# Retention of the last two batches in 64-token chunks, short units in one stretch, instruction pages in the planner, and more of v's scaling on ScalarE

## The chip, the cores and the metric

The kernel runs on one core of one Trainium2 chip. The metric is the device time of an execution in microseconds (us). The kernel before takes 283.19 us, the median of three runs (283.08 to 283.52).

The core's engines each have a queue of their own and run it in order: TensorE (PE, whose weight loads are listed apart as PEld), VectorE (DVE), ScalarE (ACT), GpSimd (POOL) and SyncE (SP). DMAs are issued from POOL, SP and ACT and are carried out by 16 DMA engines. Products of PE land in PSUM, which has eight banks; everything else is held in SBUF.

## The reference

```python
batch, n_heads, seq, head_dim = (8, 8, 576, 64)
n_tokens, d_model, d_ff = (4608, 512, 2048)

scores = scale * np.matmul(q, k.transpose(0, 1, 3, 2))      # scale = 1/sqrt(64)
gamma = 1.0 - 2.0 ** (-5.0 - np.arange(H, dtype=np.float32))
Dmat = np.where(rel >= 0, gamma[:, None, None] ** rel[None, :, :], 0.0)   # rel = pos_i - pos_j
ret = scores * Dmat[None, :, :, :]
x = np.matmul(ret, v)             # then (batch, seq, heads*head_dim) as 4608 rows of 512
h = x @ w_in
g = 0.5 * h * (1.0 + erf(h * inv_sqrt2))
out = g @ w_out
```

So there are two stages: retention (attention with a decay in place of a softmax, causal), and an MLP of two layers with an exact gelu. All inputs and the output are float32; the kernel multiplies in bfloat16 and sums in float32.

## The kernel before, in words

**Units and blocks.** The 576 tokens of a batch are four chunks of 128 and a tail of 64. A unit is one chunk of one batch; two batches make a pair (`bp`, 0 to 3), and the two units of a pair at the same chunk `ci` form a group. The tails of the two batches of a pair share one short unit. There are 36 units; four of them make a block of 512 tokens, and the MLP runs over nine blocks.

**Retention of a unit.** Because the decay is a power of the distance, a chunk needs only its own scores and a state `u` (64x64 for each head) of what came before. The steps on PE are: the transposes of q and k (the first units; later ones come by a transposing DMA from SP), `scores` (L583), `inner` (L644: masked scores times v), `state` (L673: adds k times v, scaled, to the state in PSUM), and `cross` (L690: state times q). On the other engines are `masked` (L612: scores times a mask on DVE), `scaled_v` (L630: v times a decay for each head, on DVE in one instruction or on ACT in eight), `u_copy` (L685: the state from PSUM to SBUF) and `evacuate` (L701: the result times a decay into `xT`, the MLP's input). Units with `ci` 0 (`raw`) use a full decay mask and the unscaled v, and need no cross product. With 128-token chunks the scores are a 128x128 square for each head, of which the mask removes what lies above the diagonal. With 64 rows and 64 columns to a product, PE can hold four of them in its four quarters at a time.

**The MLP.** The first layer of a block is done in four parts `kp`; three of these are "units" of seven half-size products each (a Strassen-like scheme, `unit` L957, order `PRODUCTS`) and one is plain (`mlp1` L914). `LAYOUTS` says which, and how they interleave. The second layer uses the same scheme (`fast` L972, order `SECOND`), but for block 0, which is plain. In the last block each row group `r` has its own chain of additions and its own stores (L1182): one store of half width when product 3 is in, and one of full width when products 5 and 4 are in. A store of the row group that holds the short unit goes out as two DMAs of 64 rows, since its rows belong to two batches.

**What sets the order.** The program is written straight out by a planner that runs when the kernel is built (`Plan`, L30). Each operation has a cost, a due time, dependencies, and the rings and PSUM banks that it needs; the planner keeps a clock for each engine and takes the operation that can start first. PE's work comes in three classes: single retention steps at the start, "macros" (`macro_of`, L1230: the inner, state and cross steps of a group and the scores of the next, one after the other in a stretch), and MLP pieces in between (`pe_candidates`, L1333). Groups in `APART` have their scores in a macro of their own. Up to 16 us of its own clock the planner fills gaps of PE with dummy products (`warm`, L1307). The loads are issued by POOL in the order of `ORDER`, with at most eight on their way.

**The numbers that the change touches** are the lists at L172 to L193: `VH_ACT` (units whose v is scaled on ACT; 36 and 37 name no unit), `LAYOUTS`, `ORDER`, `PRODUCTS`, `SECOND`, and the due times.

Of the kernel before, what the change touches and what calls it, by code (L numbers as in the profile page):

```python
# [9 lines left out]
FP32 = mybir.dt.float32  # L10
# [97 lines left out]
def kernel(  # L108
# [41 lines left out]
    raw = [i for i in range(N_U) if units[i][1] == 0]  # L150
    old = [0, 1, 2, 3]
    tails = list(tail_of.values())
# [6 lines left out]
    def slot_of(i):  # L159
# [12 lines left out]
    VH_ACT = [15, 18, 23, 24, 25, 34, 36, 37]  # L172
# [5 lines left out]
    VH_DUE = 14.0  # L178
    FAST = 1
    APART = [6, 7]  # L180
    BEFORE = 5.5
    UNIT_FROM = 2
    LOOK = 6
    HOLD = 5.5
    LAYOUTS = {2: ['0', '12', 'p3'], 3: ['23', '0', 'p1'], 4: ['0', '12', 'p3'], 5: ['2', '30', 'p1'], 6: ['2', '30', 'p1'], 7: ['2', '30', 'p1'], 8: ['0', '12', 'p3']}
    LEAD = 9.2
    SPREAD = 5.7
    EASE = 9
    ORDER = ("k3 v1 q3 k1 q1 wi0 v3 k2 q2 wi5 wi4 pos wi1 wi6 wi2 k5 v2 wi3 wo0 k4 q5 wi7 q4 v4 v5 wo4 v6 wo1 wo5 "
             "wo2 wo6 k6 k10 wo7 v7 k7 q8 q6 wo3 q9 q7 k9 v8 v10 k8 v9 q10").split()  # L190
    K_ORDER = [0, 1, 8, 9, 2, 3, 10, 11, 4, 5, 12, 13, 6, 7, 14, 15]
    PRODUCTS = "3251476"
    SECOND = "1267543"  # L193
# [21 lines left out]
    DRAIN = 0.21  # L215

# [106 lines left out]
    step = const.tile([128, HP, 1], FP32, name="step")  # L323
    val = const.tile([128, 1, 128], FP32, name="val")
# [50 lines left out]
    add("step", "act", 0.2, ["lg", "near7"], lambda: nc.scalar.activation(step, lgT, AF.Exp, scale=float(C)), 5.0)  # L375
    add("args", "dve", 0.45, ["pos", "lg"], make_args, 8.0)
# [6 lines left out]
    add("warm_act", "act", 1.45, ["dv", "step", *(f"dq1.{hp}" for hp in range(HP))],  # L383
        lambda: nc.scalar.activation(warm_act, ln_scale, AF.Gelu), 13.7)
    DQ = {1: [f"dq1.{hp}" for hp in range(HP)], 2: ["dq2"], 3: ["dq3"], 4: ["dq4"]}
# [114 lines left out]
    def make_dq(i):  # L500
        n = min(C, S - i * C)
        nc.vector.tensor_tensor(dqT[:, :, i * C:i * C + n], dqT[:, :, (i - 1) * C:(i - 1) * C + n],
                                step.to_broadcast([128, HP, n]), op=ALU.mult)
# [18 lines left out]
    for i in (2, 3, 4):  # L522
        add(f"dq{i}", "dve", 0.6, DQ[i - 1] + ["step"], lambda i=i: make_dq(i), (0, 0, 24.0, 34.0, 40.0)[i])

# [35 lines left out]
    def turn(i, jj):  # L560
        b, t = st[i]["tr", jj] = bank([128, HP, 128], BF16, "qk_ps")
        for hp in range(HP):
            nc.tensor.transpose(t[:, hp, :], part_of(i, jj)[0][:, 2 * hp:2 * hp + 2, :], ident1)  # L563
        read(i, f"turn{jj}")
# [17 lines left out]

    def scores(i):  # L583
        if i in old:
            qkT = qkT_of(i)
            got = [bank([128, HP, 128], FP32, f"sc{e}") for e in range(2)]
            for hp in range(HP):
                for e in range(2):
                    sl = slice(64 * e, 64 * e + 64)
                    nc.tensor.matmul(got[e][1][:, hp, :], lhsT=qkT[sl, 1, hp, :], rhs=qkT[sl, 0, hp, :],  # L590
                                     start=True, stop=True)
        elif i in tails:
            qkT = qkT_of(i)
            got = [bank([128, H, TAIL], FP32, f"sc{e}") for e in range(2)]
            for h in range(H):
                for e in range(2):
                    sl = slice(64 * e, 64 * e + 64)
                    nc.tensor.matmul(got[e][1][sl, h, :], lhsT=qkT[sl, 1, h, :], rhs=qkT[sl, 0, h, :], start=True, stop=True)  # L598
        else:
            qkT, n = qkT_of(i), i - slot_of(i)  # L600
            got = [bank([128, HP, 128], FP32, f"sc{e}") for e in range(2)]
            for hh in range(HP):
                h = 4 * n + hh
                for half in range(2):
                    out_ = slice(64 * half, 64 * half + 64)
                    for e in range(2):
                        sl = slice(64 * e, 64 * e + 64)
                        nc.tensor.matmul(got[e][1][out_, hh, :], lhsT=qkT[sl, 1, h, out_], rhs=qkT[sl, 0, h, :],  # L608
# [3 lines left out]
    def masked(i, e):  # L612
# [4 lines left out]
        rows = slice(64 * e, 64 * e + 64) if i in tails else slice(0, 128)  # L617
        shape = [128, H, TAIL] if i in tails else [128, HP, 128]
        r = st[i]["ret", e] = ret_pool.tile(shape, BF16, tag=f"ret{e}", name=f"ret{e}")
# [827 lines left out]
```

## Time and profile before

| | |
|---|---|
| median of three runs | 283.19 us |
| profiled execution | 282.95 us |
| its span, from the first to the last instruction | 281.0 us |
| PE busy | 274.9 us (98%), 3531 products |
| DVE busy | 239.2 us (85%) |
| ACT busy | 154.0 us (55%) |
| POOL busy | 110.4 us (39%) |
| granted clock of PE, mean | 0.998 |
| retention on PE: scores L608, inner L661, state L679, cross L698 | 9.0, 7.6+2.9, 6.8, 6.3 us busy |

A row of the timeline gives the start in us from the span's start, the length of the merged piece, engine, line, operation, tiles, shapes and the count of instructions; in square brackets stands how long the engine was idle before and what released it. The digits of the page are shares of busy time in 40 equal slices of 7.0 us, in tenths. Products of PE are pipelined and their ends are modelled, so lengths of neighbouring rows overlap: the time that a row takes is read from its start to the next one's start. The rows of the waits are: who waited, for whom, us in total, how many times, the longest.

### The profile page before, as it was taken

How to read it: one execution, taken by the hardware profiler on the slowest of the kernel's cores; microseconds unless marked ns; L12 is line 12 of the kernel's file. 1: busy time of each engine (PE TensorE's matmuls, PEld its weight loads, DVE VectorE, ACT ScalarE, POOL GpSimd, SP SyncE). 2: the span in 40 equal slices, each digit the busy share in tenths (PEclk: the TensorE clock that was granted, in tenths of full speed). 3: DMA queues.
4: the chain of work that ended last, by engine and by line, in shares of the span. 5: the costliest groups of instructions: out<-in, count | busy, mean ns of one | idle time of the engine just before them, and what ended most of it. 6: DMA issues, size and time to landing. Idle time of an engine off the chain costs nothing.

```text
span 281.0 us, 8429 instructions
## 1 busy us (share of the span) xinstructions
PE 274.9 (98%) x3531; PEld 220.5 (78%) x3531; DVE 239.2 (85%) x457; ACT 154.0 (55%) x339; POOL 110.4 (39%) x139
## 2 busy tenths in 40 slices
PE   7999999999999999999999999999999999999994
PEld 2589848678888688868886888688868886888783
DVE  3780693799999999999999989999999999959932
ACT  7578505455318942893188467732683458227740
POOL 8967769807946096601454713425000000000000
PEclk9999999999999999999999999999999999999999
DMA  9999999999999999999999999999900040012013
GB/s 147 161 193 180 184 179 162 190 127 200 128 150 171 196 124 123 133 220 135 165 199 89 154 146 205 48 125 147 212 1 3 2 152 2 0 51 101 2 37 112
DMA packets 152068, 35.53 MB, mean 126 GB/s; under 512 B 141024, under 2 KB 147680, under 8 KB 152032
## 3 DMA queue, kind: packets, MB, share of 16 engines
q0 software_dynamic: 115792, 17.97, 96.2%
q1 hardware_dynamic: 35200, 16.78, 32.8%
q8 instruction: 27, 0.44, 0.7%
q10 hardware_dynamic: 1040, 0.26, 0.4%
q14 instruction: 9, 0.07, 0.1%
HBM read 36.70 MB, written 9.44 MB: 164 GB/s over the span
## 4 chain that ended last, share of the span: by engine, by line
PE 92%; DVE 3%; DMA 2%; issue 0%; ACT 0%; POOL 0%; POOLq 0%
PE oT L980 33%; PE hT L920 18%; PE zT L962 10%; PE yT L962 7%; PE oT L937 5%; PE o_ps L661 3%; PE sc L608 3%; DMA qk_ld<-in_k_dram 2%; PE qk_ps L563 2%; PE u_ps L679 1%; PE warm L1312 1%; PE o_ps L698 1%; DVE s L827 1%; PE sc L590 1%; PE sc L598 0%; DVE ret L627 0%
## 5 line engine op out<-in xcount | busy, mean ns | idle before, releaser
L920 PE MATMUL hT<-xT,w_in 128*128 128x128 bf16 (+2 forms) x496 | 57.8, 269 | 0.0
L980 PEld LDWEIGHTS <-g 128*128 128x128 bf16 x512 | 49.5, 98 | 7.2
L927 ACT ACTIVATE g<-hT 128x512 bf16<-128x512 f32 (+1 forms) x76 | 38.1, 513 | 22.2 <-PE hT L920 20.6
L920 PEld LDWEIGHTS <-w_in 128*128 128x128 bf16 x496 | 37.5, 98 | 12.4
L962 PEld LDWEIGHTS <-wi_sum 128*128 128x128 bf16 x420 | 41.1, 98 | 6.4
L488 POOL DMA_DIRECT2D qk_ld<-in_q_dram x31 | 27.9, 901 | 44.1 <-DMA qkT<-qk_ld 25.0
L980 PEld LDWEIGHTS <-s 128*128 128x128 bf16 x384 | 37.1, 98 | 5.0 <-issue 0.3
L627 DVE TENSOR_TENSOR ret<-sc,msk 128x512 bf16<-128x512 f32 (+1 forms) x56 | 36.2, 680 | 1.8 <-PE sc L608 1.3
L488 POOL DMA_DIRECT2D v_ld<-in_v_dram x31 | 28.2, 911 | 10.9 <-ACT vh L640 7.2
L980 PE MATMUL oT<-w_sum,s 128*128 128x256 bf16 x256 | 31.1, 273 | 0.2 <-ACT o_sb L1068 0.2
L1068 ACT COPY o_sb<-oT 128x512 f32<-128x512 f32 (+1 forms) x27 | 14.4, 539 | 29.7 <-PE oT L980 16.2
L980 PE MATMUL oT<-w_sum,g 128*128 128x256 bf16 x256 | 30.6, 273 | 0.0
L488 POOL DMA_DIRECT2D qk_ld<-in_k_dram x31 | 28.3, 912 | 4.4 <-DMA v_ld<-in_v_dram 2.3
L980 PE MATMUL oT<-w_out,g 128*128 128x256 bf16 x256 | 29.8, 273 | 0.0
L1037 ACT ACTIVATE g<-zT 128x512 bf16<-128x512 f32 x42 | 24.3, 610 | 2.2 <-DVE zT L1046 1.5
L1072 DVE TENSOR_TENSOR o_sb<-o_sb,oT 128x512 f32<-128x512 f32 (+1 forms) x27 | 16.7, 623 | 9.5 <-ACT o_sb L1068 5.4
L538 DVE COPY qkT<-qk_ps 128x512 bf16<-128x512 bf16 x17 | 6.8, 419 | 17.3 <-PE qk_ps L563 17.2
L637 DVE TENSOR_TENSOR vh<-v_ld,dv 128x512 bf16<-128x512 bf16 x30 | 20.2, 681 | 1.5 <-DMA v_ld<-in_v_dram 1.5
L962 PEld LDWEIGHTS <-w_in 128*128 128x128 bf16 x168 | 16.4, 98 | 2.1
L540 ACT COPY q<-yT 128x512 f32<-128x512 f32 x13 | 7.5, 593 | 17.3 <-PE yT L962 17.3
L716 DVE TENSOR_TENSOR xT<-o_ps,dqT 128x512 bf16<-128x512 f32 x24 | 15.3, 679 | 0.5 <-PE o_ps L698 0.5
L937 PE MATMUL oT<-w_out,g 128*128 128x512 bf16 x64 | 15.5, 380 | 0.0
(175 smaller groups left out, 472.4 us busy)
## 6 DMA issues: line engine op xcount, KB each, us to landing
out_dram<-o_sb SPq DMA_DIRECT2D x30, 256.0 KB, 3.2
qk_ld<-in_k_dram POOLq DMA_DIRECT2D x31, 128.0 KB, 6.8
v_ld<-in_v_dram POOLq DMA_DIRECT2D x31, 128.0 KB, 7.8
qk_ld<-in_q_dram POOLq DMA_DIRECT2D x31, 128.0 KB, 6.8
w_in<-in_moe_w_in_dram POOLq DMA_DIRECT2D x8, 256.0 KB, 8.5
w_out<-in_moe_w_out_dram POOLq DMA_DIRECT2D x8, 256.0 KB, 8.2
out_dram<-o_sb SPq DMA_DIRECT2D x12, 128.0 KB, 2.8
qk_ld<-in_k_dram POOLq DMA_DIRECT2D x8, 64.0 KB, 6.5
```

The source lines that it names most:

```text
L488: nc.gpsimd.dma_start(dst, src[2 * bp + j, :, ci * C:ci * C + C, :].rearrange("h s d -> s h d"))
L627: nc.vector.tensor_tensor(r[rows], t[rows], by, op=ALU.mult)
L637: nc.vector.tensor_tensor(vh, loaded[i][1], dv[:, :, ci:ci + 1].to_broadcast([128, H, D]), op=ALU.mult)
L716: nc.vector.tensor_tensor(dst, o, dqT[:, :, ci * C:ci * C + C], op=ALU.mult)
L920: nc.tensor.matmul(hT[:, m, :], lhsT=w[:, cc, o:o + 128], rhs=x_of(t)[:, cc, lo:hi], start=(cc == 0), stop=(cc == N_DM - 1))
L927: nc.scalar.activation(g_of(t, m0)[:, m0 % 2:m0 % 2 + n, m0 // 8, lo:hi], hT, AF.Gelu)
L937: nc.tensor.matmul(oT, lhsT=g_of(t, m)[:, m % 2, m // 8, ts * 128:ts * 128 + 128], rhs=w_out_sb[m // 2][:, m % 2, :], start=(n == 0), stop ...
L962: nc.tensor.matmul(c[:, m, :], lhsT=unit_left(kp, p, m)[:, cc, :], rhs=unit_right(t, p)[:, cc, :], start=(p in "321" and m + cc == 0), sto ...
L980: nc.tensor.matmul(c[:, at, :], lhsT=left(t, p, kp)[:, kk, r * 128:r * 128 + 128], rhs=right(p, kp)[:, kk, :], start=(p in OPENS and at + ...
L1037: nc.scalar.activation(target(key, what), chain[key][n][1], AF.Gelu)
L1068: nc.scalar.copy(target(key, what), chain[key][n][1])
L1072: nc.vector.tensor_tensor(to, to, chain[key][n][1], op=ALU.add)
```

## The change

1. *Fine units.* The units of the last batch pair (`FINE = 3`) are worked in two halves of 64 tokens. Scores, inner, cross and state products are all 64x64 with 64 columns; the half above the diagonal is left out. The state is copied twice a chunk: after the first half (`u..,0`) and after the second (`u..,1`). Each chunk is two macros: (a) the inner products between the two halves, the first half of the state update and half of the next group's scores, (b) the inner products within each half, all cross products, the second half of the state update and the other half of the next group's scores. `weave` writes the products of two lists, one for the upper and one for the lower 64 rows of the array, in turn. Between macros the planner keeps `GAP_A` or `GAP_B` of 1.6 us. A chunk needs two masks in place of four. Chunk 0 of this pair is no longer `raw`: its v is the scaled one, it is evacuated by DVE with a decay table `dq0`, which one more instruction on each of ACT and DVE makes.
2. *Short units* have one bank for their scores and one mask; inner and cross are one woven stretch (`in_t`).
3. *Pages.* The planner counts products; every 127.8 of them it holds PE's clock until 3.5 us (6.2 while the planner has a DMA moving) after the last page began.
4. *ScalarE scales v* of 20 units in place of 6, each in four parts of two heads in place of two parts of four.
5. The lists are others: `ORDER` (the position table of POOL third, unit 1's k and v behind the first weights), `LAYOUTS` (three parts by the seven-product scheme and one plain in every block, as before), `PRODUCTS` and `SECOND` with the last two exchanged, and due times.

```diff
+    FINE = 3
+    fine = [i for i in range(N_U) if units[i][0] >= FINE and units[i][2] is not None]
+    raw = [i for i in range(N_U) if units[i][1] == 0 and i not in fine]
...
-    VH_ACT = [15, 18, 23, 24, 25, 34, 36, 37]
+    VH_ACT = [5, 6, 7, 8, 9, 10, 16, 17, 19, 20, 23, 25, 27, 29, 30, 31, 32, 33, 34, 35, 36, 37]
...
+    PARTS = 4
     FAST = 1
+    FETCH = 3.5
+    BUSY_FETCH = 6.2
+    GAP_A = 1.6
+    GAP_B = 1.6
     APART = [6, 7]
-    BEFORE = 5.5
+    BEFORE = 3.7
     UNIT_FROM = 2
     LOOK = 6
-    HOLD = 5.5
-    LAYOUTS = {2: ['0', '12', 'p3'], 3: ['23', '0', 'p1'], 4: ['0', '12', 'p3'], 5: ['2', '30', 'p1'], 6: ['2', '30', 'p1'], 7: ['2', '30', 'p1'], 8: ['0', '12', 'p3']}
-    LEAD = 9.2
-    SPREAD = 5.7
+    HOLD = 5.0
+    LAYOUTS = {2: ['0', '12', 'p3'], 3: ['0', '12', 'p3'], 4: ['01', '2', 'p3'], 5: ['01', '2', 'p3'], 6: ['23', '0', 'p1'], 7: ['0', '12', 'p3'], 8: ['0', '12', 'p3']}
+    LEAD = 8
+    SPREAD = 6.7
     EASE = 9
-    ORDER = ("k3 v1 q3 k1 q1 wi0 v3 k2 q2 wi5 wi4 pos wi1 wi6 wi2 k5 v2 wi3 wo0 k4 q5 wi7 q4 v4 v5 wo4 v6 wo1 wo5 "
-             "wo2 wo6 k6 k10 wo7 v7 k7 q8 q6 wo3 q9 q7 k9 v8 v10 k8 v9 q10").split()
+    ORDER = ("q1 q2 pos k2 q3 k3 v3 wi0 k1 wi4 v2 v1 wi5 wi1 wi2 wi3 wi6 v4 k5 wi7 q5 q4 wo0 k4 v5 wo4 wo1 wo5 wo2 "
+             "q9 wo6 q6 wo7 v10 v7 q8 k7 v6 wo3 k6 v9 q7 k10 k9 v8 k8 q10").split()
...
-    PRODUCTS = "3251476"
-    SECOND = "1267543"
+    PRODUCTS = "3251467"
+    SECOND = "1267534"
...
+    PAGE, PAGE_AT = 127.8, 92
+    page = [0, 0.0]
+
+    def paged():
+
+        while made[0] > PAGE_AT + page[0] * PAGE:
+            T["pe"] = max(T["pe"], page[1] + (BUSY_FETCH if any(m.start <= T["pe"] < m.end - 1.0 for q_ in moving.values() for m in q_) else FETCH))
+            page[:] = page[0] + 1, T["pe"]
...
+    def scores_atoms(n, b):
+        qkT, sc, rows = qkT_of(n), st[n]["sc", b][1], half(b)
+        if n in tails:
+            return [(N64, [(sc[rows, h, :], qkT[rows, 1, h, :], qkT[rows, 0, h, :], True, True)]) for h in range(H)]
+        return [(N64, [(sc[half(t), h, :], qkT[rows, 1, h, half(t)], qkT[rows, 0, h, half(t)], True, True) for t in range(2)])
+                for h in range(H)]
...
+    def weave(names):
...
+        order, took = [], 0.0
+        for r, atoms in enumerate(lists_of(names)):
+            at = 0.0
+            for lasts, products in atoms:
+                order.append((at, r, products))
+                at += lasts
+            took = max(took, at)
+        waits_for = {fences[nm] for nm in names if nm in fences}
+        for n, (_, _, products) in enumerate(sorted(order, key=lambda o: o[:2])):
+            for out_, w, x, begin, ends in products:
+                last_on_pe[0] = product(out_, lhsT=w, rhs=x, start=begin, stop=ends, skip_group_check=True)
+                for one in waits_for:
+                    tc.add_manual_dep(last_on_pe[0].ins, one, SYNC, reason="row tiles take turns at a bank")
+                waits_for = ()
+        return took
...
+    def masked(n, b):
+
+        at, t = st[n]["sc", b]
+        if ("ret", 1) not in st[n]:
+            ret_ring.take()
+        r = st[n]["ret", b] = ret_pool.tile([128, H, 64], BF16, tag=f"ret{b}", name=f"ret{b}")
+        nc.vector.tensor_tensor(r, t, msk2.to_broadcast([128, H, 64]), op=ALU.mult)
+        release(at, T["dve"] + 0.12)
...
+    def u_copy(bp, ci, t, engine):
+        ins = (nc.vector.tensor_copy if engine == "dve" else nc.scalar.copy)(u_sb[t if bp >= FINE else ci % 2], u_bank[1])
+        if t == 0:
+            tc.add_manual_dep(ins.ins, last_on_pe[0].ins.name, SYNC, reason="row tiles take turns at a bank")
+            fences[f"in_b{pair_of[bp, ci][0]}"] = ins.ins.name
...
-            add(f"vha{i}", "act", 1.05, before, lambda i=i: scaled_v(i, "act", (0, 4)), due, at=room)
-            add(f"vh{i}", "act", 1.05, [f"vha{i}"], lambda i=i: scaled_v(i, "act", (4, 8)), due + 0.5)
+            step_ = H // PARTS
+            for p in range(PARTS):
+                name = f"vh{i}" if p == PARTS - 1 else f"vh{i}.{p}"
+                add(name, "act", 0.2625 * step_, [f"vh{i}.{p - 1}"] if p else before,
+                    lambda i=i, p=p, step_=step_: scaled_v(i, "act", (p * step_, p * step_ + step_)), due + p / PARTS, at=None if p else room)
...
+        back, front = groups[n - 1], groups[n] if n < len(groups) and n not in APART else []
+        states = states_behind(n - 1)
+        if back[0] in fine:
+            a = [f"in_a{back[0]}"] + [f"st_a{bp},{ci}" for bp, ci in states]
+            b = [f"in_b{back[0]}"] + [f"st_b{bp},{ci}" for bp, ci in states]
+            if front:
+                a, b = a + [f"odd_{front[0]}"], b + [f"even_{front[0]}"]
+            return [a, b]
+        ahead = scores_of(front)
+        olds = [f"state{bp},{ci}" for bp, ci in states]
+        if back[0] in tails:
+            return [olds + [f"in_t{back[0]}"] + ahead]
+        return [[f"inner{i}" for i in back] + olds + ahead + [f"cross{i}" for i in back if units[i][1]]]
...
+                at = max(at, stretch_end[0] + (GAP_B if ops[0].startswith("in_b") else GAP_A))
```

## The prediction

> **What bounds the kernel now.** I read the page first, then the waits of TensorE (PE), then PE's order of time at four places: the start, a retention stretch of the last batch pair, the last short unit, the end.
>
> ```profile
> span 281.0 us, 8429 instructions
> ...
> PE 274.9 (98%) x3531; PEld 220.5 (78%) x3531; DVE 239.2 (85%) x457; ACT 154.0 (55%) x339; POOL 110.4 (39%) x139
> ...
> PE   7999999999999999999999999999999999999994
> DVE  3780693799999999999999989999999999959932
> ...
> DMA  9999999999999999999999999999900040012013
> ...
> q8 instruction: 27, 0.44, 0.7%
> ```
>
> PE is busy from the second slice to the last but one, at nines. DVE is nearly as full, ACT half empty, and the DMA engines go quiet after slice 29 (203 us). The waits of PE:
>
> ```profile
> PE warm L1320 <- DVE ln_scale L320: 1.2, 1, 1.2
> PE qk_ps L563 <- DMA qk_ld<-in_k_dram: 0.3, 1, 0.3
> PE oT L980 <- ACT o_sb L1068: 0.2, 1, 0.2
> ```
>
> After the start PE waits 0.2 us in all. So DVE, full as it is, delays nobody, and three things alone can move the end: PE's own work, the start (filled with dummy "warm" products), and what follows the last product. The start:
>
> ```profile
> 12.89 0.61 PE L920 MATMUL hT<-xT,w_in 128*128 128x128 bf16 x8
> 13.33 1.08 PE L1312 MATMUL warm<-u_sb 128*128 128x512 bf16 x5
> 14.35 0.41 PE L661 MATMUL o_ps<-ret,v_ld 128*64 128x128 bf16 x8
> ...
> 15.71 0.87 PE L1312 MATMUL warm<-u_sb 128*128 128x512 bf16 x4
> 16.41 0.61 PE L920 MATMUL hT<-xT,w_in 128*128 128x128 bf16 x8
> ```
>
> The first product of the MLP starts at 12.89; the last dummies are at 15.71, and from 16.41 on PE has real work. A stretch of the last pair, then the last short unit:
>
> ```profile
> 216.44 0.64 PE L661 MATMUL o_ps<-ret,vh 128*64 128x128 bf16 x16
> 216.91 0.42 PE L679 MATMUL u_ps<-vh,qk_ld 128*64 128x64 bf16 x16
> 217.26 0.64 PE L608 MATMUL sc<-qkT 64*64 64x128 bf16 x32
> 217.73 0.39 PE L698 MATMUL o_ps<-qkT,u_sb 64*64 64x128 bf16 x16
> 218.06 0.61 PE L980 MATMUL oT<-w_sum,s 128*128 128x256 bf16 x4
> ...
> 243.72 0.32 PE L653 MATMUL o_ps<-ret,vh 64*64 64x64 bf16 x16
> 243.86 0.30 PE L698 MATMUL o_ps<-qkT,u_sb 64*64 64x64 bf16 x16
> 244.09 1.05 PE L980 MATMUL oT<-w_sum,s 128*128 128x256 bf16 x8
> ```
>
> First start to the MLP's next start: 1.62 us for 80 products of a chunk, 0.37 for 32 of a short unit. In the trace's start times the first product comes 0.09 later than the MLP's pace, so these cost 1.71 and 0.46. The end:
>
> ```profile
> 277.01 0.42 DVE L1072 TENSOR_TENSOR o_sb<-o_sb,oT 128x256 f32<-128x256 f32 x1 [0.45 <-PE oT L980]
> ...
> 274.84 3.10 SPq L1124 DMA_DIRECT2D out_dram<-o_sb  x5
> ```
>
> The last addition ends at 277.43; of the five stores the last is issued at 277.55 and lands at 279.52; closing waits take the span to 281.0.
>
> **The change, part by part.** I sum against this execution: 282.95 us, 281.0 of it span; it lies 0.24 below the median, 283.19, to which I add the sum.
>
> *64-token retention (batches 6 and 7).* In the short unit, four 64x64 products start together every 32 ns. The stretch is 8 such fours, 0.25, plus 0.22 that does not depend on length (0.09 in, 0.02 at the first four, 0.10 out). Every woven stretch of the changed kernel is made of such fours. Chunk 0: (a) first inner half, state half, half the scores = 12 fours, 0.38+0.22 = 0.60; (b) the rest = 16 fours, 0.72. Chunks 1 to 3 have 20 fours in (b), 0.85. Before: 183.08 (previous short unit with the first scores) 0.92, 188.38 1.48, 209.48 and 216.44 1.71 each, 236.97 1.51, 243.72 0.46: 7.79. After: 16 fours 0.72, then 0.60+0.72, three times 0.60+0.85, and 0.47: 6.86. That is 0.93 less. The count of products rises (80 to 128 a chunk), the fours fall.
>
> *Short units in one stretch.* At 69.98 the unit's inner and cross products stand around a state update with 128 rows, 0.96 in all; put together they save one switch between tile shapes, 0.10 to 0.14 by the trace's start times there. I take 0.14. The other short units keep their switches. PE's work: -1.07.
>
> *DVE and ACT.* DVE loses 14 scalings of v (0.68 each), 8 masks of the fine units and 4 of short units (0.68), and gains two evacuations, one table and up to four state copies: net about -13 us. Nothing waits for DVE, so this is worth 0. ACT gains 14x8 small scalings, 0.245 apart in the trace: +27 on 154 of 281 us. It is hidden as long as a v is ready some microseconds ahead (1.96 on ACT instead of 0.68): priced at 0; if the cover is gone, 1.3 us for each v that is late, and the gelus queued behind a part wait up to 0.5.
>
> *The new wait.* Between (a) and (b) one engine copies the state: 0.2 for the products to drain, 0.6 to 0.7 of copy, 0.2 of signals, about 1.1; the plan puts 1.6 us of MLP between. Behind a late copy stand (b) and all MLP products in order. Bounds 0 and 0.5 for each of four chunks; I take 0, nearest to the 0.2 that PE waits today under the same planner.
>
> *Load order and the start.* Loads land 0.88 us apart, weight blocks 1.33, from 7.60 on (landing times in the trace), since the DMA engines are full. New order: q1 q2 k2 q3 k3 v3, then wi0 at about 13.2, k1 14.1, wi4 15.4, v2 16.3, v1 17.1. POOL's position table moves up past nine loads and delays each by 0.26 of issue, covered by the 0.88. Today, when PE has real work for good (16.41), it has done 8 transposes (1.8 us), 3 scores and 3 inners (2.0), one MLP piece (0.45): 4.25, so 12.1 lost. With the new order units 0 and 3 are through at wi0 and wi4, unit 2 about 1.1 after its v: at 17.45 PE has done 8 transposes, 4 scores, 3 inners, 4 pieces, 5.9, so 11.5 lost. That is -0.6; bounds +0.5 (a mask later by one) and -1.5.
>
> *The end.* With the second layer's last product 4 instead of 3, the last store is no longer 128 rows of half a width but the short unit's rows of full width: two issues, one behind the other. Today's pair for the same rows goes out at 275.72 and 276.24 and lands 2.93 after the first issue; the single last store lands 1.97 after its own. +0.9; bounds 0 and 1.1.
>
> *Instruction pages.* 27 pages of 0.44 MB for 7062 PE instructions: 16 KB, some 130 products with their weight loads. Today a page lasts at least 5 us (80 products of a chunk, 1.7, and fifty at 0.109), and PE never waits. In the fine chunks (a), 1.6 us of MLP and (b) make a page in 3.05. A page's transfer takes 0.7% of 16 engines' span over 27, 1.2 us; small stores land 2.8 after issue, loads on the full queue 6.8. Bounds: 0 and 3.75 a chunk. I take 0.1 in all, since three of the four chunks come after slice 29, when the queue is quiet and 2.8 is below 3.05.
>
> [...]
>
> Sum: -1.07 -0.6 +0.9 +0.1 = -0.67, so 282.5.
>
> **Rivals.**
> 1. *Issue limits the short products* (other side). The densest long row today is 183.08: 64 products in 0.72 without its way out, 11.3 ns each; 32 ns a four is shown for 32 products only. At 11.3 the stretches of 40 to 80 products take 0.07 to 0.27 more each, 1.7 together: 284.2, slower. It decides from about 9.3 ns a product, where the gain of 0.67 is gone. For: nothing today is longer at that density. Against: the eight fours show no slowing.
> 2. *Page stalls.* If a page needs the plan's own quiet figure, 3.5 us, and PE is through in 3.05, four chunks cost 1.8 instead of 0.1: 284.2; one chunk among running loads up to 3.75 more. For: full queue at 183. Against: none today, and the plan can place a chunk elsewhere in a page.
> 3. *The start gains nothing*: x of units 1 and 2 comes a mask later. 283.1, no change.
> 4. *More gain*: the start reaches 1.3 and the last two stores overlap better (0.4 of the 0.9 gone): 281.4. For: the table of gelu is loaded earlier, as POOL's positions come third; today the first gelu waits until 15.63 for it.
>
> **How the numbers follow.** A measurement here tells 0.2%, 0.57 us, from no change. Forecast 0.42, its own range 282.0 to 283.0, two thirds of it below 282.6; rival 1 0.10, rival 2 0.13, rival 3 0.13, rival 4 0.22. Faster 0.28+0.22 = 0.50; same 0.14+0.13 = 0.27; slower 0.23. The range runs from rival 4 to rival 1, 281.4 to 284.2, leaving out most of rival 2's loaded case and the lowest of rival 4.
>
> **What would show it.** Right: a fine chunk as two stretches of 0.60 and 0.85; no wait of PE after the start; PE's real work from about 17.5 with more pieces ahead of it; the last landing 2.9 after the first issue of the last pair. Wrong: a hole of over 0.3 us inside a stretch with no releaser (pages), fours further apart than 32 ns (issue), PE waiting for a state copy or for v on ACT, or dummies after 18 us.

## The result and the profile after

The changed kernel takes 284.61 us, the median of eight runs (283.85 to 285.15); the kernel before, run beside it, 283.34 us (283.08 to 283.94, eight runs). The ratio is 1.0038 with an interval of 1.0023 to 1.0054: slower by about 0.4%, where 282.5 and "faster" had been forecast. (All ratios and intervals below come from runs made beside runs of the kernel before on the same chip; they can differ by some 0.1% from the quotient of two medians.)

The profiled execution of the changed kernel took 285.15 us, the longest of its eight; that of before took 282.95, less than any of the eight. So the two traces lie 2.2 us apart, 0.9 more than the medians; where that comes from is seen below. First the page of the changed kernel:

```profile
span 283.2 us, 8896 instructions
...
PE 274.2 (97%) x3707; PEld 219.8 (78%) x3721; DVE 224.5 (79%) x430; ACT 182.7 (65%) x458; POOL 110.3 (39%) x139
...
DVE  5760392689999997999799998986997788769832
...
q8 instruction: 29, 0.48, 0.8%
```

DVE lost 14.7 us and ACT gained 28.7, as announced (-13 and +27). PE's busy time fell by 0.7 only. (14 products of the 3721 have no record, as the count of weight loads shows; a gap of exactly one product's length, in which the weight load stands, is such a record and no wait.) The waits of PE:

```profile
PE warm L229 <- DVE ln_scale L347: 1.2, 1, 1.2
PE oT L229 <- issue: 0.8, 2, 0.7
PE zT L229 <- ACT g L1209: 0.4, 2, 0.2
PE qk_ps L233 <- DMA qk_ld<-in_q_dram: 0.3, 1, 0.3
PE o_ps L229 <- PE sc L229: 0.3, 1, 0.3
```

Three rows are new. PE waited 0.8 us for "issue", that is for nothing that a semaphore shows; 0.68 of it is one hole, and the rest, at 58.9, stands beside a product without a record. It waited twice for ACT's gelu `g`. The last row, a product waiting for PE's own scores, lies at 13.55, in the start. Measured against PE's own pace (a product of 256 columns every 0.109 us), what PE loses to waits after 18 us is 0.39 us before and 2.04 after. One fine chunk in the timeline (start, length, operation; read from start to start):

```profile
218.26 0.60 PE L229 MATMUL oT<-w_sum,g 128*128 128x256 bf16 x4
218.79 0.22 PE L229 MATMUL u_ps<-vh,qk_ld 64*64 64x64 bf16 x2
218.80 0.22 PE L229 MATMUL o_ps<-ret,vh 64*64 64x64 bf16 x2
218.85 0.20 PE L229 MATMUL u_ps<-vh,qk_ld 64*64 64x64 bf16 x2
...
219.30 1.05 PE L229 MATMUL oT<-w_sum,g 128*128 128x256 bf16 x8
...
221.15 0.32 PE L229 MATMUL o_ps<-ret,vh 64*64 64x64 bf16 x16
221.30 0.43 PE L229 MATMUL o_ps<-qkT,u_sb 64*64 64x64 bf16 x32
...
221.96 0.61 PE L229 MATMUL oT<-w_sum,s 128*128 128x256 bf16 x4
```

Part (a) takes 0.51 from first start to the MLP's next start, part (b) 0.81; with the 0.09 by which the first product comes late, 0.60 and 0.90. Before, the chunk was one stretch of 1.71. The hole, and a gelu that comes late:

```profile
192.36 1.16 PE L229 MATMUL oT<-w_sum,s 128*128 128x256 bf16 x9
...
194.19 0.93 PE L229 MATMUL oT<-w_sum,s 128*128 128x256 bf16 x7 [0.68 <-issue]
194.19 0.86 PEld L229 LDWEIGHTS <-s 128*128 128x128 bf16 x8 [0.85 <-issue]
```

```profile
115.06 0.69 DVE L568 COPY t<-yT 128x512 f32<-128x512 f32 x1
...
115.84 0.60 ACT L1209 ACTIVATE g<-yT 128x512 bf16<-128x512 f32 x1 [0.55 <-DVE t L568]
...
116.34 0.59 ACT L1209 ACTIVATE g<-zT 128x512 bf16<-128x512 f32 x1
...
116.98 0.60 PE L229 MATMUL zT<-xs,wi_sum 128*128 128x256 bf16 x4 [0.21 <-ACT g L1209]
```

In the first fence the last of nine products, 0.109 apart, starts at 193.24; the next product starts at 194.19 in place of 193.35, and its weight load waits just as long, with no releaser. In the second, DVE copies the bank `yT` to `t`, and ACT's gelu of the same bank starts only when that copy is through; the second gelu, of `zT`, is then late, and PE's product into the freed `zT` starts 0.37 late against its pace. The end:

```profile
276.44 3.73 SPq L1296 DMA_DIRECT2D out_dram<-o_sb  x5
...
278.61 0.42 DVE L1244 TENSOR_TENSOR o_sb<-o_sb,oT 128x256 f32<-128x256 f32 x1 [0.45 <-PE oT L229]
```

After the last addition, which ends at 279.03, two stores go out at 279.06 and 279.58 and land at 281.31 and 281.95. From the start of the last product to the end of the span it is 4.86 us; before, 4.26.

The 2.2 us between the traces, term by term (us):

| term | forecast | measured, after less before |
|---|---|---|
| fine chunks: 7.05 in place of 7.80 | -0.93 | -0.75 |
| short unit at 69: 0.84 in place of 0.96 | -0.14 | -0.12 |
| waits for a late gelu, at 117.0 and 231.1 | 0 | +0.74 |
| other waits of PE: 0.46 after, 0.39 before | 0 | +0.1 |
| page: hole at 193.24 | +0.1 | +0.84 |
| start, up to 22 us | -0.6 | +0.8 to +1.0 |
| end | +0.9 | +0.6 |
| sum | -0.67 | +2.2 |

"Start" is what PE lost up to 22 us (the time less its work at full pace): 13.10 before and 14.12 after, of which 0.8 is needed to close the sum. Three terms are thus open: the gelus, the hole, and the start.

### The profile page after: what moved, and what is told of

Read it like the earlier page. It is cut to its first block, busy times and chain, and to the rows that moved or that the text cites. A ratio compares the mean times of both kernels' runs of the same rounds, so it can differ in the third digit from the quotient of the medians.

```text
span 283.2 us, 8896 instructions
## 1 busy us (share of the span) xinstructions
PE 274.2 (97%) x3707; PEld 219.8 (78%) x3721; DVE 224.5 (79%) x430; ACT 182.7 (65%) x458; POOL 110.3 (39%) x139
## 4 chain that ended last, share of the span: by engine, by line
PE 78%; DMA 11%; POOL 6%; issue 2%; ACT 1%; DVE 1%; POOLq 0%; ACTq 0%
PE oT L229 37%; PE hT L229 11%; PE zT L229 9%; DMA w_in<-in_moe_w_in_dram 6%; PE yT L229 6%; PE o_ps L229 4%; POOL qk_ld L517 3%; DMA w_out<-in_moe_w_out_dram 3%; PE sc L229 3%; PE u_ps L229 2%; DMA qk_ld<-in_k_dram 2%; POOL v_ld L517 1%; ACT g L1209 1%; PE qk_ps L233 1%; DVE t L568 0%
## 5 line engine op out<-in xcount | busy, mean ns | idle before, releaser
L229 PEld LDWEIGHTS <-g 128*128 128x128 bf16 x576 | 54.9, 98 | 12.5
L229 PE MATMUL hT<-xT,w_in 128*128 128x128 bf16 (+2 forms) x488 | 56.1, 267 | 0.4
L229 PE MATMUL oT<-w_out,g 128*128 128x256 bf16 (+1 forms) x315 | 44.0, 293 | 0.2 <-issue 0.2
L824 ACT ACTIVATE vh<-v_ld,dv 128x64 bf16<-128x64 bf16 x160 | 44.0, 344 | 0.0
L652 DVE TENSOR_TENSOR ret<-sc,msk 128x512 bf16<-128x512 f32 x36 | 23.0, 680 | 0.9 <-PE sc L229 0.9
L570 ACT COPY q<-yT 128x512 f32<-128x512 f32 x17 | 9.9, 590 | 18.3 <-PE yT L229 18.3
L855 DVE TENSOR_TENSOR xT<-o_ps,dqT 128x512 bf16<-128x512 f32 x26 | 16.7, 680 | 3.0 <-PE o_ps L229 3.0
L568 DVE COPY qkT<-qk_ps 128x512 bf16<-128x512 bf16 x16 | 6.2, 418 | 15.4 <-PE qk_ps L233 15.4
L1218 DVE TENSOR_TENSOR zT<-q,zT 128x512 f32<-128x512 f32 x21 | 14.5, 692 | 1.6 <-PE zT L229 1.4
L829 ACT CAST u_sb<-u_ps 128x512 bf16<-128x512 f32 x15 | 8.8, 584 | 10.7 <-PE u_ps L229 7.1
```

Of the source, the lines that this page charges most:

```text
L229: return nc.tensor.matmul(*args, **more)
L570: nc.scalar.copy(dst, src)
L652: nc.vector.tensor_tensor(r, t, by, op=ALU.mult)
L824: nc.scalar.activation(vh[:, h], loaded[i][1][:, h], AF.Copy, scale=dv[:, h, ci:ci + 1])
L829: ins = (nc.vector.tensor_copy if engine == "dve" else nc.scalar.copy)(u_sb[t if bp >= FINE else ci % 2], u_bank[1])
L855: nc.vector.tensor_tensor(dst, o, dqT[:, :, ci * C:ci * C + C], op=ALU.mult)
```

## The experiments

### The start: order of the loads, or something else

Three explanations stood against each other. The position table, third in the new order, could delay the loads behind it; the planner's idea of when PE becomes fast (`HOT`, 9.2) could be wrong for the new order; or the start could differ from run to run, whatever the order. First the table alone, moved behind unit 1's v (e1), and the whole old order in the changed kernel (e5):

```diff
-    ORDER = ("q1 q2 pos k2 q3 k3 v3 wi0 k1 wi4 v2 v1 wi5 ...
+    ORDER = ("q1 q2 k2 q3 k3 v3 wi0 k1 wi4 v2 v1 pos wi5 ...
```

> The changed kernel with one item of its load order moved: POOL's position table stands behind v1 (twelfth, about where it stood before) and not third. Theory A (the early table lets the planner put the decay tables and the scaling of v ahead of unit 0's masks on DVE and ACT, so that the first MLP product comes late): first MLP product back near 13.2 us, last dummy product 0.5 to 1 us of dead time less, time 0.5 to 0.9 us below the changed kernel's 284.6. Rival (the order of the loads itself, weights behind six unit loads, makes the start late): first MLP product stays near 15, time within 0.3 us of 284.6.

> The changed kernel with the old order of loads. Theory S (the start costs the changed kernel some 0.9 us, because unit 0 gets through later and products at half clock fill the wait): the first MLP product back at about 12.9 us, real work for good from about 16.4, time 0.5 to 1.0 us below 284.6. Rival (the clock of PE rises at a moment that the order of loads does not set, so the start's loss is chance from run to run): first MLP product anywhere between 12.9 and 15.4 and time within 0.4 of 284.6.

Measured: e1 284.82 us, ratio 1.0048 (1.0030 to 1.0066); the first MLP product came at 14.17 where it was 14.99, and PE lost 13.90 up to 22 us where it was 14.12. So the table isn't what delays the start. e5: 283.76 us, 1.0026 (1.0013 to 1.0039), with its first MLP product at 13.88 and a loss of 14.06, and no page hole. The old order brought the start no gain, and took none from it; the little that the time fell by is less than the missing hole (below).

The reason shows when executions with the same start are compared. The kernels e10 and e16 (below) both have the old order, and PE does the same products in the same order at their start. Their timelines, e10 first:

```profile
11.22 0.40 PE L233 MATMUL qk_ps<-ident,qk_ld 128*128 128x128 bf16 x4
11.55 0.40 PE L229 MATMUL sc<-qkT 64*128 64x128 bf16 x8
11.88 0.56 PE L229 MATMUL warm<-u_sb 128*128 128x512 bf16 x4
...
12.82 0.61 PE L229 MATMUL hT<-xT,w_in 128*128 128x128 bf16 x8
```

```profile
12.31 0.61 PE L233 MATMUL qk_ps<-ident,qk_ld 128*128 128x128 bf16 x4
12.85 0.61 PE L229 MATMUL sc<-qkT 64*128 64x128 bf16 x8
13.39 0.92 PE L229 MATMUL warm<-u_sb 128*128 128x512 bf16 x4
...
14.70 0.61 PE L229 MATMUL hT<-xT,w_in 128*128 128x128 bf16 x8
```

The same four transposes take 0.33 from their start to the next row's in e10 and 0.54 in e16. Until some moment PE runs at half pace (128 columns in 107 ns, 512 in 427 ns), and then at full pace (56 and 216 ns in the trace of before). The row PEclk of every page shows nines in all slices meanwhile, so the page doesn't show it; the lengths of the rows do, and so do the throttle's own entries in the packed trace: the first of them, a grant of the full clock, stands at 9.2 in e10 and at 14.2 in e16, and the time before it, which has no entry, counts as full on the page. Over all executions with the old order the moment lies between these (10.2 and 11.1 in two of the unchanged kernel), with the new order between 10.5 and 13.8 (12.8 in the profile of after). A wait for the loads doesn't explain it: e5 and e10, with the same products and the same gap of 0.21 before the transposes at 7.6, have it 3.6 us apart (12.8 and 9.2).

What PE loses up to 22 us follows that moment, at 0.4 to 0.5 us for each us: 13.02 at 9.2 and 14.84 at 14.2 with the old order; 12.90 at 10.5 and 14.55 at 13.8 with the new one. Lines through nine points of the old order and eight of the new (e1 and e8, which change the start itself, left out) give, at 11.7, 13.7 for the old order and 13.6 for the new, and 14.1 for both at 12.8: the new order saves some 0.1 and not 0.6, and single points of the old order lie up to 0.3 off their line. So the moment, 12.8 in one trace and 10.2 in the other, is enough for the start's +0.8 to +1.0 between them. (e1, with its moment at 11.3, lost 0.5 more than the new order's line has there; a late table does not help.) The moments also span enough (5.0 us, 1.8 us of time) to cover the spread of both kernels' runs; that they cause it was not shown.

PE has products from 1.19 us on in the traces of before and after, with no idle time over 0.32 us until it becomes fast, at 10.2 in the one and at 12.8 in the other; over the runs the moments lie 5.0 us apart. The 1.8 us by which the loss differs between the earliest and the latest are 0.6% of the span, and that is more than the change as a whole moved.

A planner that knows the later moment was tried (e8), and the new order in a calm plan (e20, which is e7 below with the new `ORDER`):

```diff
-    HOT = 9.2
+    HOT = 13.0
```

> The changed kernel whose planner counts PE at half speed up to 13.0 us of its clock in place of 9.2, so that it fills the gaps before 13 us with half as many dummy columns. Theory H (products at half clock up to 11 to 14 us make the dummies twice as long as planned and push unit 0's products back): unit 0's inner product, at 13.55 us in the changed kernel, comes at 12 us or before, the first MLP product before 14 us, time 0.5 us below 284.6. Rival (masks or loads hold unit 0): inner product not before 13, time unchanged.

> The kernel of the new parts with old lists (282.6 us, PE's waits 0.06 us) with the new load order alone. By the prediction's working of the start 0.6 less: 282.0. By the runs so far (time lost up to 22 us follows the moment when the clock rises, and at the same moment the new order loses 0.1 to 0.25 less): 282.4 to 282.5, not to be told from 282.6. If the order changes the later plan: 283 or more, with waits after 18 us.

e8: 286.05 us, 1.0097 (1.0071 to 1.0123). A miss for the time, but not for the start:

```profile
12.98 0.60 PE L229 MATMUL sc<-qkT 64*128 64x128 bf16 x8
13.51 0.45 PE L229 MATMUL warm<-u_sb 128*128 128x128 bf16 x2
13.79 0.61 PE L229 MATMUL hT<-xT,w_in 128*128 128x128 bf16 x8
```

The scores at 12.98 still take 0.53 where eight at full pace take 0.33; the full clock comes at 13.4. The loss up to 22 us was 13.47, 0.9 less than the new order's line has at that moment (14.4), and unit 0's inner product came at 12.41 where it was 13.55. So a planner that counts with the slow pace does start better, as theory H had it, in the one profile that there is. But PE's waits after 18 us rose to 3.5 with the other plan, and the time with them. e20: 283.10 us, 0.9985 (0.9965 to 1.0004), against 0.9975 for e7: no gain from the order, and two waits of 0.49 and 0.22 that e7 has not.

### The hole at 193.24: a page of instructions

The place of the hole, counted in pairs of weight load and product, is the same in the profiles of after, e1, e2 and e10: just after pair 2646 (in e6 after pair 2648). The planner's own page count, 92 and 20 pages of 127.8, gives 2648 for a page's beginning. If the hole belongs to the pages, it must stay at that count when the program gets longer ahead of it, and so move to other products; a wait for data would stay with its products. Eight of the first dummy products were cut in four (24 pairs more) and, in another kernel, in eight (56 more), which leaves the planner's times as they are:

```diff
-        product(t, lhsT=zeros[:, :128], rhs=zeros, start=True, stop=True)
+        for part in range(4):
+            nc.tensor.matmul(t[:, part * 128:part * 128 + 128], lhsT=zeros[:, :128], rhs=zeros[:, :128], start=True, stop=True)
+        made[0] += 1
```

> The changed kernel with each of the eight first dummy products (512 columns) cut into four of 128: same columns, same plan, but 24 more PE instruction pairs, so every instruction page ends 24 products earlier. Theory P (the 0.84 us hole at 193.2 us with no releaser is PE out of instructions, since a page was used up in 3.9 us after the last one began): the hole goes or moves to another place where two short stretches lie inside a page; time about 0.8 us less if it goes. Rival (the hole is a wait for data, or a property of the short stretches): the hole stays at the same product with 0.8 us.

> The changed kernel with each of the eight first dummy products cut into eight of 64 columns: 56 more PE instruction pairs, so that pair 2646, where the hole lies, falls 56 products earlier in the program, ahead of the stretch at 189 us, with MLP products between it and the page before. Theory P: no hole at pair 2646, and none elsewhere if no other page is used up in under 4 us; time 0.4 to 0.9 below 284.6 (the hole measured 0.36 to 1.02 in five runs). Rival: a hole of that size at the same place in the program.

e3: 284.88 us, 1.0067 (1.0037 to 1.0098). The hole is again after pair 2646, which is now 24 products earlier, in the middle of a fine stretch:

```profile
191.11 0.32 PE L229 MATMUL o_ps<-ret,vh 64*64 64x64 bf16 x16
...
191.51 0.19 PE L229 MATMUL sc<-qkT 64*64 64x64 bf16 x1
192.55 0.19 PE L229 MATMUL sc<-qkT 64*64 64x64 bf16 x1 [0.85 <-issue]
...
192.80 1.05 PE L229 MATMUL oT<-w_sum,s 128*128 128x256 bf16 x8
```

That stretch costs 1.78 in place of 0.76. e18: 284.12 us, 1.0021 (1.0005 to 1.0036): no hole anywhere, and the other waits as after (0.19, 0.18, 0.38 and 0.37 at the same products). The hole is shown to be a page's. It is worth 0.84 in the trace of after, but it differs from execution to execution (0.36 in e1, 0.54 in e2), and by the medians, 284.61 and 284.12, about half a us; the two intervals overlap.

Its size can be read too. The instruction queue's DMA of that page ran from 191.17 to 192.76 after, and PE went on at 194.19, 1.43 later; in e1, e2, e3 and e10 it is 1.36, 1.51, 1.43 and 1.46, and in e6 1.20. Where the transfer came earlier there was no hole: in e5 it was in at 190.03, in e7 at 189.79. After, PE used that page up in about 3.9 us (from about 189.4 to 193.24) and would have needed 4.8; the planner holds PE for 3.5 when it sees no transfer, and 6.2 when it sees one. At 190 to 193 the DMA engines are at nines in the trace. Which of its two figures the planner used there was not looked at.

At the other 28 of the changed kernel's 29 pages no hole shows; at this one it was 0.36 to 1.11 us in six kernels.

### The end: the order of the last products

```diff
-    SECOND = "1267534"
+    SECOND = "1267543"
```

> The changed kernel with the old order of the second layer's products (3 last again, so that the last store is one DMA of half width). If the end costs what the traces say (4.86 us from the last product's start to the end of the span, 4.26 before), the tail shrinks by 0.6 us and the time falls to about 284.0; if the second layer's order matters elsewhere too, PE gets waits of its own in the middle and the time does not follow the tail.

Measured: 283.65 us, 1.0004 (0.9988 to 1.0019). From the last product's start to the end it is 4.03 where it was 4.86. That is -0.83 in the trace and about -0.96 by the medians, more than the 0.6 expected. The old order's last store is one issue of 128 rows; the new one's are two of 64, one behind the other.

### Fine units, in the new plan and in a calm one

```diff
-    FINE = 3
+    FINE = 4
```

> The changed kernel with 128-token chunks for the last two batches again (FINE = 4: no unit is fine), all else as changed. Theory (retention of that pair is 0.75 us shorter on PE in 64-token chunks, and the page hole of 0.84 is its price): stretches at 1.71 and 1.49 us again, no hole near 193, the time within 0.3 us of 284.6. Rival (64-token chunks save nothing that counts, the hole is the whole loss): 283.8. Rival (they pay in full): 285.3.

e4: 286.58 us, 1.0118 (1.0099 to 1.0137), 2 us above what was expected. The plan without fine units has waits of its own, 3.1 us in all, the longest of them these:

```profile
PE yT L229 <- DVE xs L1054: 0.7, 1, 0.7
PE zT L229 <- DVE q L1188: 0.6, 1, 0.6
```

So one part undone in the changed kernel tells little of that part: every edit makes the planner write another program. The parts were therefore tried from the other side, each added to a plan with few waits. That plan is the changed kernel with all lists of before (e7): the fine units, the one-stretch short units and the page clock stay.

```diff
 ORDER, VH_ACT, LAYOUTS, BEFORE, HOLD, LEAD, SPREAD, PRODUCTS, SECOND: as in the kernel before
```

> The changed kernel's new parts (64-token chunks for the last pair, short units in one stretch, pages in the planner, v in parts of two heads) with every list and due time of the kernel before: VH_ACT, LAYOUTS, ORDER, PRODUCTS, SECOND, BEFORE, HOLD, LEAD, SPREAD. If the lists lose and the new parts win, as the ledger of the two traces says (retention -0.87, rest +2.1): 282.4 to 282.9. If the new parts themselves lose (page holes, waits for the state's copy): 283.7 or more.

> The kernel of the new parts with all old lists (282.6 us), but with 128-token chunks for the last pair (FINE = 4). If the 64-token chunks are worth what their stretches on PE say (0.75 us) in a plan without other waits: 283.4, the level of the kernel before less 0.1 for the short unit. If their gain is more than PE's stretches (DVE's masks): 284 or more. If none: 282.6.

e7: 282.62 us, 0.9975 (0.9963 to 0.9986), faster than both kernels, and the fastest of all that were run. Its waits:

```profile
PE warm L229 <- DVE ln_scale L347: 1.2, 1, 1.2
PE qk_ps L233 <- DMA qk_ld<-in_k_dram: 0.3, 1, 0.3
PE hT L229 <- ACT g L1209: 0.2, 1, 0.2
```

After 18 us PE loses about 0.6, all of it behind gelus (0.28 in the stretch before 125.56, 0.22 at 233.35), and the end is 4.02. (The expectations of e12 and e20 say 0.06, which leaves these two out. The one at 233.35 is as long as a product, but no record is missing here: the trace has 3723 weight loads and 3723 products.) e14, which is e7 with `FINE = 4`: 283.05 us, 1.0001 (0.9988 to 1.0014). The fine units are worth 0.43 us in a calm plan by the medians and 0.7 by the ratios; 0.75 had been expected from their stretches. So the code of the change gains, and the lists lose it.

### Which list: ScalarE's share, the layouts, or the orders

Three orders were put back in the changed kernel (e10: `ORDER`, `PRODUCTS`, `SECOND`); `VH_ACT` alone was put back (e6); and in e7 the new `VH_ACT` alone (e12) or the new layouts and due times alone (e13) were put in:

```diff
-    VH_ACT = [15, 18, 23, 24, 25, 34, 36, 37]
+    VH_ACT = [5, 6, 7, 8, 9, 10, 16, 17, 19, 20, 23, 25, 27, 29, 30, 31, 32, 33, 34, 35, 36, 37]
```

> The changed kernel with the old load order, the old order of products and the old second layer, but the new VH_ACT, LAYOUTS and due times. If start (0.9), end (0.6 to 0.8) and the two waits of 0.37 us for a gelu at 116 and 230 us come from these three: 282.3 to 282.8, below both kernels. If the waits come from work that has moved to DVE and ACT instead, they stay somewhere and the time is 283.0 or more.

> The changed kernel with the old VH_ACT (6 units scaled on ACT in place of 20). If VH_ACT carries the loss in the changed kernel too: PE's waits after 18 us, 2.2 us with the page hole, fall below 1.0, time 283.3 or less. Rival (the other new lists lose by themselves, as the load order and the second layer): 284 or more.

> The kernel of the new parts with all old lists (282.6 us), with the new VH_ACT alone: 20 units' v scaled on ACT. Theory V (it is work moved to ACT, and what DVE takes over from ACT in turn, that makes PE wait for gelus and for sums of x): PE's waits after 18 us rise from 0.06 to 0.7 us or more, time 283.2 or more. Rival L (the new LAYOUTS and due times make the waits): waits stay below 0.3 and the time at 282.6.

> The kernel of the new parts with all old lists (282.6 us), with the new LAYOUTS, BEFORE, HOLD, LEAD and SPREAD alone. Theory V: waits of PE after 18 us below 0.3 us, but for a page hole where one falls, time 282.6. Rival L: 0.7 us or more of waits, 283.2 or more.

e10: 283.19 us, 1.0003 (0.9987 to 1.0020), with the hole (0.80), a wait of 0.47 for DVE and one of 0.42 for a gelu: the waits stay with the other lists. e6: 286.09 us, 1.0090 (1.0067 to 1.0114), slower than the changed kernel, a miss; it has a hole of 1.11 and new waits of 0.4 to 0.5 at 76.3, 155.6 and 209.2. e12: 284.96 us, 1.0061 (1.0034 to 1.0087), 2.3 above e7. e13: 282.90 us, 0.9990 (0.9981 to 1.0000), 0.3 above e7 with waits of 1.2. In the calm plan it is `VH_ACT` that costs, and the waits of e12 say how:

```profile
PE zT L229 <- ACT g L1209: 1.0, 4, 0.3
PE oT L229 <- DVE ret L652: 0.3, 1, 0.3
PE yT L229 <- DVE xs L1054: 0.3, 1, 0.3
```

Each of the four follows the pattern seen after, a gelu held back by a copy; in two of them (123.68 and 207.42) two parts of v stand between the two gelus besides. From e12's timeline:

```profile
142.88 0.69 DVE L568 COPY t<-yT 128x512 f32<-128x512 f32 x1
...
143.66 0.60 ACT L1209 ACTIVATE g<-yT 128x512 bf16<-128x512 f32 x1 [0.55 <-DVE t L568]
...
144.16 0.59 ACT L1209 ACTIVATE g<-zT 128x512 bf16<-128x512 f32 x1
...
144.80 0.60 PE L229 MATMUL zT<-xs,wi_sum 128*128 128x256 bf16 x4 [0.21 <-ACT g L1209]
```

The copy `t<-yT` may be done by either engine, and the planner gives it to the one that its clocks say is free. DVE gets 7 of 21 in the kernel before and in e7, 8 after, 10 in e12; with ACT doing more of v's scaling that tends to rise, but it is the planner's choice each time (e1, with the same new `VH_ACT` as after, has 4, and no late gelu). On ACT the copy and the gelu of the bank follow each other without a signal; on DVE the gelu waits for the copy, 0.5 to 0.6 us of idle time on ACT, and the planner's model lets the two run side by side. Gelus with that wait of 0.49 or more: none in e7 (one of 0.27), one before (232.21, where PE lost 0.06), two after, five in e12. So it counts less how many copies DVE has than whether the gelu comes up right behind one. To test it, the copy is tied to ACT in e12, with `VH_ACT` as in e12:

```diff
-            add(nm + "raw", "any", acts, pe["5"], lambda engine: raw12(key, width, engine), ...
+            add(nm + "raw", "act", acts["act"], pe["5"], lambda: raw12(key, width, "act"), ...
```

> The kernel of the new parts and old lists with the new VH_ACT (284.96 us), and the copy of product 5's bank (t, of the seven-product scheme) given to ACT always, where the planner chose ACT or DVE before. Theory T (ACT's gelu of that bank waits about half a us for DVE's copy, which the planner does not know, and product 7 waits for ACT): PE's four waits of 1.0 us for a gelu vanish, time 283.9 or less. Rival (ACT is simply too full with 160 small scalings and the gelus wait behind them): the waits stay or grow, since ACT gets ten copies more, time 285 or more.

e16: 283.09 us, 0.9985 (0.9970 to 1.0000). The gelu's waits are gone, and after 18 us PE loses 0.69 where it was 2.17 in e12 and another 0.5 inside stretches. The same place in its timeline:

```profile
143.70 0.57 ACT L570 COPY t<-yT 128x512 f32<-128x512 f32 x1
...
144.17 0.60 ACT L1209 ACTIVATE g<-yT 128x512 bf16<-128x512 f32 x1
...
144.66 0.60 ACT L1209 ACTIVATE g<-zT 128x512 bf16<-128x512 f32 x1
144.68 1.04 PE L229 MATMUL zT<-xT,wi_sum 128*128 128x256 bf16 x8
```

By the ratios, tying the copy to ACT takes 0.76% or 2.1 us off; what is left of the larger `VH_ACT`'s cost, 0.1%, is within the intervals. In the trace of e12 the gelus' four waits are 1.65 us of that. Another 0.4 is a wait for a mask on DVE, in the stretch at 161, which went too; whether the copy or the new plan took that one away isn't shown.

In both places shown with the copy on DVE, `g<-yT` starts 0.09 after the copy's end, though both only read the bank; what puts the two in order was not looked into.

### The kernel before once more, and three causes undone together

The kernel before was profiled a second time (e15), and the changed kernel was run with the copy `t` on ACT, the old `SECOND`, and the dummies cut in eight (e19); everything else of the change stays.

> The kernel before once more, for the start alone. If the moment at which PE's products fall from half to full clock is chance, it lies elsewhere than the 10.1 us of the first profile (between 9.4 and 13.9 in the runs so far), and the time lost up to 22 us with it; if the order of loads sets it, it is 10.1 again.

> The changed kernel with the three causes taken away together: t copied by ACT always, the old second layer (3 last), and the pages shifted by 56 pairs. If they add up (waits for gelus 0.75, end 0.84, hole about 0.5 by the clock of the runs): about 282.5, below the kernel before. If the planner, whose order changes with t's engine, makes other waits: above 283.

e15, one run: 283.31 us, PE fast from 11.1 where it was 10.2, first MLP product at 13.18, loss 13.38 up to 22 us: 0.3 from the first profile in the start alone. e19: 282.70 us, 0.9982 (0.9968 to 0.9996) beside 283.55 for the kernel before. Its waits after 18 us are 0.67, its end 4.05, and neither a hole nor a late gelu is left. The changed kernel is 0.38% slower than before; with these three undone it is 0.18% faster. So these three are the causes of the loss. They give 0.56%, 1.6 us, together, where 2.1 had been expected from the parts; the two intervals, of 0.15% to either side each, leave room for that. The gelus alone were not undone in the changed kernel, and tying the copy to ACT makes another plan, as every edit here does.

## Why the prediction was wrong

**Retention, -1.07: right in kind, -0.87 measured.** Fours of 64x64 products do start about 32 ns apart over 80 products, and (a) is 0.60 to the hundredth. (b) took 0.90, 0.90 and 0.86 in place of 0.85, the stretches of 16 fours 0.76 in place of 0.72; what the 0.01 to 0.05 are wasn't looked into. e14 against e7 gives 0.43 for the fine chunks by the medians and 0.7 by the ratios, where the stretches have 0.75.

**"Nothing waits for DVE, so this is worth 0. ... It is hidden" (ACT): this step failed.** The cover that was named, v ready some microseconds ahead, held: no v was late. What was missed is that the planner deals the raw copies out anew when ACT's and DVE's work changes, and that a gelu on ACT stands still behind a copy that it gave to DVE. It cost 0.74 in the trace of after; in e12 the four gelus cost 1.65, and tying the copies to ACT brought 2.1. That the copy costs is shown by e16 and e19; that in the changed kernel `VH_ACT` brought it about, and not another list, is not shown, since undoing `VH_ACT` there (e6) gave another plan with a late gelu of its own. The price "the gelus queued behind a part wait up to 0.5" had the right size for one gelu, but mostly another cause.

**Instruction pages, +0.1: wrong step.** The page was taken to be needed 2.8 us after its predecessor in a quiet stretch. 193 us lies in slice 28, where the queue is still full, PE used the page up in 3.9 us rather than 3.05, and it would have needed 4.8, of which 1.4 pass after the page has landed. This is the "one chunk among running loads" of rival 2: the cause was named and given a chance of 0.13, the size up to 3.75; it was 0.84.

**Start, -0.6: wrong step.** Landing times and masks were added up from one execution, in which PE became fast at 10.2. That moment lies between 9.2 and 14.2, differently in executions of the same start, and moves the loss by 0.4 to 0.5 us for each us; at the same moment the new order gains about 0.1. The nearest was rival 3, "the start gains nothing", for another reason.

**End, +0.9: right for the exchange of the two products.** 0.83 in the trace and 0.96 by the medians against the same kernel with the old order. Against the kernel before it is 0.6, since the new code's end with the old order is 4.03 and not 4.26; where these 0.23 come from stays open. **New wait for the state copy, 0: right**; no wait of PE names `u_sb`.

**Rival 1** (issue limits the short products) fell: (b) takes 0.81 for 80 products where 11.3 ns each would make 0.90 without its way out; the fours stay about 32 ns apart.

Without the chance in the start the loss is then: -0.87 for retention, +0.6 for the end, +0.74 for the gelus, +0.5 to +0.84 for the page, and about -0.1 for the start, together +0.9 to +1.2. The ratio's interval is 0.65 to 1.5 us.

What stays open: what sets the moment at which PE becomes fast; when a page is asked for, and what passes in the 1.2 to 1.5 us after the landing; why the plans of e4, e6 and e8 have 3 us of waits, which was only read from their waits and not tested.

## What to carry to other kernels

Where a planner writes the program, a forecast has to ask of every freed engine what the planner will give it next, and who stands behind that: a large part of the loss here came from a copy that nobody edited. To price one part, add it alone to the calmest plan there is; taking it out of a plan with several troubles gives another plan with other troubles (e4, e6 and e8 were all slower than what they were taken from). And before the starts of two traces are compared, find the moment in each at which PE's rows halve in length, since that alone moved a start by 1.8 us here.

## What the runs showed of the hardware that was not expected

PE goes on 1.20 to 1.51 us after the DMA of an awaited page of instructions has landed (six profiles), so a page is late well before its transfer is. PE runs at half pace (128 columns in 107 ns, later in 56) from its first products until 9.2 to 14.2 us into the span, differently in executions of the same start, while the row of the granted clock shows full speed. And 160 PE instructions, weight loads and 64x64 products in turn, were issued in 0.81 us without a gap, at 5 ns each.
